# First tile of x in two channel halves, with offsets per stage and tile in the planner's ranks

## The chip, the cores and the metric

The kernel runs on one core of a Trainium2 chip. The metric is the device time of one execution in microseconds (us). The core has five engines, each with its own in-order instruction queue: TensorE (PE) for matrix products, VectorE (DVE) and ScalarE (ACT) for elementwise work, GpSimd (POOL), and SyncE (SP), which here only issues DMA transfers. PE writes to PSUM, and VectorE and ScalarE read it from there.

## The reference

A small neural speech codec: a depthwise convolution over time with three taps, SiLU, a residual vector quantiser with four codebooks of eight entries, and a second depthwise convolution over the sum of the chosen entries. `x` is 2 x 16000 x 512, in bf16.

```python
xp = jnp.pad(x, ((0,0),(pad,pad),(0,0)))
for i in range(K):                                  # K = 3
    z = z + xp[:, i:i+T, :] * dw_enc[i][None, None, :]
z = _silu(z)
res = z
for s in range(Nq):                                 # Nq = 4, C = 8 entries each
    cb = codebooks[s]
    d2 = |res|^2 - 2.0 * res @ cb.T + |cb|^2
    sel = cb[d2.argmin(-1)]
    q = q + sel
    res = res - sel
for i in range(K):
    y = y + qp[:, i:i+T, :] * dw_dec[i][None, None, :]
```

(The line for `d2` is written shorter here; `qp` is `q` padded like `xp`.)

## The kernel before

The 2 x 16000 time steps are cut into 18 tiles, numbered 0 to 17: 6, 8 and seven times 16 groups of 128 time steps for the first sequence, seven times 16, then 8 and 6 groups for the second. Time step and group are interleaved (`"(p g) d -> g p d"`), so that group g holds every G-th step, and the neighbour in time of a whole group is the group beside it. Channels lie on partitions: the 512 channels are four blocks of 128 (`KT` = 4).

**Loading** (`load`, L487). Every group is brought in by one transposing DMA from SyncE's queue (L493), 128 steps by 512 channels (128 KB), into slot g + 1 of the tile `XT[n % 2]`. Slots 0 and G + 1 are the halo: the last and the first group shifted by one step. For tiles inside a sequence they are two more transposing loads (L501, L507). For tile 0 both are made on GpSimd: a memset and a copy of slot G into slot 0 (L504), and a memset and a copy of slot 1 into slot G + 1 (L510). There are two `XT` buffers, so the loads of tile n + 2 come after the taps of tile n.

**Taps and SiLU** (`front`, L514, `front2`, L542). Each tile is worked in two channel halves h (blocks 0, 1 and 2, 3). Each half has six tap products `TA`/`TB` from `XT` and `WENC` (L531 on ScalarE or L532 on VectorE), two sums on VectorE (recorded at the helper's line, L364), exp on ScalarE (L537), plus one (L538 or L539), reciprocal on ScalarE (L549) and the gate `ZB * EX` on VectorE. The list `allx` (L524) names what a half's taps read; before, it is every slot of the tile.

**Selection** (`select`, L582; `resid`, L681). PE forms the products of z with the codebooks and with itself (L567); VectorE takes the scores (L601, L602) and decides three codebooks in a chain of small operations, with a PE transpose (L639), a copy of it (L643 on ScalarE or L644 on VectorE) and a correction on PE (L649) between them. The one-hot rows are transposed on PE (L672) and copied into `OHW` (L678, either engine). `resid` then subtracts the chosen entries from z in 24 pieces per tile. A piece taken by VectorE is one product group on PE (L701) and one add of PSUM to `ZB` (L709). A piece taken by ScalarE also needs `ZB` itself through an identity product (L700), and then one copy (L707). The fourth codebook follows (L725, L726, small operations, L672, L678).

**Back** (`back`, L741). PE multiplies the one-hot windows with prepared decoder weights (L758 to L762), ScalarE copies PSUM to `YB` (L766), and SyncE stores it (L789).

**Setup** (`setup`, L366) makes the constants with many short operations; up to the first tap VectorE is busy with them for 9.82 us, and the rest (decoder weights `WDEC`, L485, among it) lies between the work of tiles 0 and 1.

**The order.** Every step is registered with `add` under an engine (or both VectorE and ScalarE), a cost in us, a key of stage, tile number and place, and what it reads and writes. `Plan.order` (L75) simulates the engines with these costs. Again and again it takes the step that can start first; ties go to the smaller `rank` (L55), made of the tile number and two weights per stage in `WHEN`. There is one pair of weights each for tiles 0 to 2, 3 to 14 and 15 to 17 (`part`, L52). The result is the program order of all engines; `fill` (L807) puts filler products into PE where the plan sees it idle. Four things decide which engine a step gets:

- `SHARE`: a residual piece goes to VectorE if VectorE's load plus SHARE is below ScalarE's (L126).
- `QUOTA`: how many PSUM boxes may be held for an engine at a time (L120, L127). Score products also hold one for VectorE.
- `SLACK`: a step that both can do goes to ScalarE only if ScalarE would end no later than VectorE's end plus SLACK (L132).
- `LATENCY` and the PSUM banks' free times, from which the plan's waits follow.

These costs shape the order only; on the chip the queues wait for what they need.

## Time and profile before

| | |
|---|---|
| median of 8 runs (lowest to highest) | 732.79 us (728.52 to 735.04) |
| profiled execution: time, span | 731.26 us, 729.5 us |
| busy VectorE, ScalarE, PE (of which fillers, L809) | 674.8, 658.5, 590.6 us (72.8) |
| PE clock granted, mean | 0.967 |
| transposing loads, output stores (DMA instructions) | 283, 130 |
| issue of one transposing load, of one store (median) | 1.26 us, 0.36 us |
| first tap of tile 0, of tile 2 | 13.10 us, 52.35 us |
| last work of VectorE, of PE, of ScalarE | 719.8, 721.7, 724.1 us |

All times within the kernel count from the start of the span. A line such as "L709 DVE TENSOR_TENSOR ZB<-ZB,ps" is a group of instructions: source line, engine, operation, what is written from what, shapes and count; then the busy time, the mean duration of one in ns, and the engine's idle time just before them with what ended most of it. In a timeline the two first numbers are start and duration in us, and a bracket gives the idle time before. "SPq" is SyncE's queue issuing.

### The profile page before, as it was taken

The numbers are of one execution on the slowest core, as the hardware profiler recorded it, in microseconds if no ns is written. First come the engines' busy times: TensorE is split into PE (matmuls) and PEld (weight loads), VectorE is DVE, ScalarE is ACT, GpSimd is POOL, SyncE is SP. The second block draws the span as 40 slices with busy tenths as digits, with TensorE's granted clock in tenths as the row PEclk, the third lists the DMA queues.
The fourth block names the chain that finished last, engine by engine and source line by source line (L and its number), as shares of the span: only waits on it lengthen the run. The fifth ranks groups of instructions, "written<-read, shape, count | busy, mean of one in ns | idle before, by whom it ended". The sixth has DMA issues, their size and how long they took to land.

```text
span 729.5 us, 24386 instructions
## 1 busy us (share of the span) xinstructions
PE 590.6 (81%) x10725; PEld 288.4 (40%) x10725; DVE 674.8 (93%) x1258; ACT 658.5 (90%) x583; POOL 10.7 (1%) x35
## 2 busy tenths in 40 slices
PE   5977676887897886888788778877888897889995
PEld 2443243343443443434344334433344343444442
DVE  8779899999999999999998999999999999999993
ACT  6888998699999999899989999999899999999666
POOL 2000000000010000000000000000000010000000
PEclk9999799999999999999999999989999999999999
DMA  5454556624155353736634434542535130302316
GB/s 110 95 99 91 94 117 91 144 67 95 30 147 95 102 90 99 121 79 139 112 103 101 139 74 109 132 83 66 90 119 138 56 121 22 119 2 88 118 31 212
DMA packets 163968, 71.89 MB, mean 99 GB/s; under 512 B 155567, under 2 KB 155599, under 8 KB 163862
## 3 DMA queue, kind: packets, MB, share of 16 engines
q1 hardware_dynamic: 163646, 69.90, 41.3%
q8 instruction: 84, 1.38, 0.8%
q10 hardware_dynamic: 216, 0.43, 0.3%
q14 instruction: 22, 0.18, 0.1%
HBM read 0.43 MB, written 32.77 MB: 46 GB/s over the span
## 4 chain that ended last, share of the span: by engine, by line
DVE 51%; PE 26%; issue 8%; ACT 7%; SPq 6%; DMA 2%; DVEq 0%; ACTq 0%
DVE ZB L709 11%; PE ps L701 7%; DVE ZB L364 7%; DVE TA L364 7%; DVE TB L532 6%; PE ps L700 6%; SPq L493 6%; PE ps L567 4%; DVE TA L532 3%; PE ps L758 3%; DVE EX L539 2%; ACT YB L766 2%; DVE OHW L678 2%; PE ps L809 2%; ACT ZB L707 2%
## 5 line engine op out<-in xcount | busy, mean ns | idle before, releaser
L701 PE MATMUL ps<-OHW,CBN 128*128 128x512 bf16 (+1 forms) x768 | 267.2, 385 | 20.0 <-DVE ZB L709 10.3
L707 ACT CAST ZB<-ps 128x1024 bf16<-128x1024 f32 (+2 forms) x296 | 253.6, 932 | 31.5 <-PE ps L701 29.6
L700 PE MATMUL ps<-ZB,IDENT 128*128 128x512 bf16 (+1 forms) x530 | 205.5, 388 | 32.1 <-ACT ZB L707 14.0
L709 DVE TENSOR_TENSOR ZB<-ZB,ps 128x1024 bf16<-128x1024 bf16 (+2 forms) x136 | 143.2, 1065 | 3.9 <-PE ps L701 3.3
L701 PEld LDWEIGHTS <-CBN 128*128 128x128 bf16 x768 | 74.6, 99 | 142.4 <-issue 75.9
L766 ACT CAST YB<-ps 128x1024 bf16<-128x1024 f32 x126 | 121.8, 1044 | 9.4 <-PE ps L762 4.5
L537 ACT ACTIVATE EX<-ZB 128x4096 bf16<-128x4096 bf16 (+2 forms) x36 | 115.1, 3197 | 8.9 <-DVE ZB L364 8.6
L549 ACT ACTIVATE EX<-EX 128x4096 bf16<-128x4096 bf16 (+2 forms) x36 | 114.7, 3195 | 0.2
L567 PEld LDWEIGHTS <-ZB 128*32 128x32 bf16 x8064 | 75.3, 95 | 54.9 <-issue 52.7
L532 DVE TENSOR_SCALAR TB<-XT,WENC 128x2048 bf16<-128x2048 bf16 (+2 forms) x139 | 92.8, 686 | 0.2
L567 PE MATMUL ps<-ZB 128*32 128x64 bf16 x8064 | 87.6, 198 | 6.5 <-issue 4.2
L758 PE MATMUL ps<-WDEC,OHW 128*128 128x512 bf16 x252 | 74.0, 387 | 13.0 <-DVE ZB L709 4.6
L809 PE MATMUL ps<-MSK,IDENT 128*128 128x512 bf16 x294 | 72.8, 397 | 14.3 <-DVE RC L617 2.4
L700 PEld LDWEIGHTS <-IDENT 128*128 128x128 bf16 x530 | 52.8, 100 | 66.9 <-issue 14.7
L364 DVE TENSOR_TENSOR ZB<-ZB,EX 128x4096 bf16<-128x4096 bf16 (+2 forms) x36 | 72.7, 2022 | 3.6 <-ACT EX L549 3.6
L364 DVE TENSOR_TENSOR TA<-TA,TB 128x4096 bf16<-128x4096 bf16 (+2 forms) x36 | 72.8, 2022 | 1.0 <-ACT TB L531 0.6
L364 DVE TENSOR_TENSOR ZB<-TA,TB 128x4096 bf16<-128x4096 bf16 (+2 forms) x36 | 73.0, 2026 | 0.1
L532 DVE TENSOR_SCALAR TA<-XT,WENC 128x2048 bf16<-128x2048 bf16 (+2 forms) x70 | 46.9, 689 | 0.9 <-DMA out_dram<-YB 0.4
L809 PEld LDWEIGHTS <-IDENT 128*128 128x128 bf16 x294 | 28.7, 101 | 47.2 <-issue 19.2
L539 DVE TENSOR_SCALAR EX<-EX 128x4096 bf16<-128x4096 bf16 (+2 forms) x35 | 38.5, 1099 | 2.0 <-ACT EX L537 2.0
L758 PEld LDWEIGHTS <-OHW 128*128 128x128 bf16 x252 | 22.8, 98 | 41.3 <-issue 18.2
L561 PE MATMUL ps<-MSK,IDENT 128*128 128x512 bf16 (+1 forms) x64 | 24.5, 383 | 8.3 <-ACT ZB L707 2.4
(100 smaller groups left out, 401.5 us busy)
## 6 DMA issues: line engine op xcount, KB each, us to landing
out_dram<-YB SPq DMA_DIRECT2D x33, 448.0 KB
out_dram<-YB SPq DMA_DIRECT2D x28, 512.0 KB
XT<-in_x_dram SPq DMA_TRANSPOSE x283
out_dram<-YB SPq DMA_DIRECT2D x30, 60.0 KB
out_dram<-YB SPq DMA_DIRECT2D x31, 2.0 KB
out_dram<-YB SPq DMA_DIRECT2D x2, 224.0 KB
YB<-in_dw_dec_dram ACTq DMA_DIRECT2D x1, 384.0 KB
out_dram<-YB SPq DMA_DIRECT2D x1, 384.0 KB
```

The lines of the kernel that those rows point to most:

```text
L364: add("DVE", cost, key, lambda: nc.vector.tensor_tensor(out=out, in0=a, in1=b, op=op), reads, writes, **kw)
L532: lambda dst=dst, src=src, w=w: nc.vector.tensor_scalar(out=dst, in0=src, scalar1=w, scalar2=None, op0=ALU.mult),
L537: add("ACT", act(2 * R), ("exp", n, h), lambda: nc.scalar.activation(v(ex), Z, ACT.Exp, scale=-1.0), zt, [("EX", sl), "ACTTAB"], hold="E")
L549: nc.scalar.add_instruction(mybir.InstActivation(name=nc.get_next_instruction_name(), engine=mybir.EngineType.Activation, func=ACT.Reciprocal,
L567: nc.tensor.matmul(o[HB * q:HB * (q + 1), u * ZW:(u + 1) * ZW].rearrange("p (s c) -> p s c", s=2), lhsT=blk, rhs=both, start=False, stop=( ...
L700: nc.tensor.matmul(o, lhsT=IDENT, rhs=zg[:, k0:k0 + nk, :], start=True, stop=False)
L701: nc.tensor.matmul(o, lhsT=CBN[s, u][:, i * P:(i + 1) * P], rhs=W[:, k0:k0 + nk, PADC:PADC + P], start=not on_act, stop=True)
L707: nc.scalar.copy(zg, v)
L709: nc.vector.tensor_tensor(out=zg, in0=zg, in1=v, op=ALU.add)
L758: nc.tensor.matmul(o, lhsT=W[:, k, PADC:PADC + P], rhs=WDEC[u], start=True, stop=not wrap)
L766: add("ACT", act_psum(1024), key, lambda k=k, box=box, Y=Y, k0=k0: nc.scalar.copy(Y[:, 2 * (k - k0):2 * (k - k0) + 2, :].rearrange("p g d ...
L809: nc.tensor.matmul(PS[j // 2][:, 512 * (j % 2):512 * (j % 2) + NMK * ZW], lhsT=IDENT, rhs=MSK.rearrange("p u w -> p (u w)"), start=True, s ...
```

## The change

`load` takes tile 0 in two parts of two channel blocks each. For each part the load of slot G comes first, then slots 1 to G - 1, then both halo memsets and copies of that part; the second part follows the first. The tokens that order the steps now name slot and channel block, so that a half's taps depend on the loads of their own two blocks. For the other tiles the loads are as before. The planner gets the margins `MARGIN` (added to the latency behind PE, in front of PE and to the freeing of PSUM banks; a factor on the cost of products) and the table `NUDGE` with an offset per stage and tile, added to the ranks, to SHARE and to SLACK. `SHARE`, `SLACK`, `QUOTA` and `WHEN` have new values. What is computed is the same.

```diff
--- before.py
+++ after.py
@@ -27,9 +27,10 @@
     SPAN, BUSY = 3.413, 0.5
     GATE = {"resid": (1.0, 2.0), "back": (1.0, 2.0), "win0": (0.6, 1.5), "win3": (0.6, 1.5), "score0": (0.25, 1.4), "score3": (0.25, 1.4)}
 
-    def __init__(self, pairs, edges, share, slack, quota, when):
+    def __init__(self, pairs, edges, share, slack, quota, margin, when, nudge):
         self.steps, self.writer, self.readers = [], {}, {}
-        self.pairs, self.edges, self.share, self.slack, self.quota, self.when = pairs, edges, share, slack, quota, when
+        self.pairs, self.edges, self.share, self.slack, self.quota, self.margin, self.when = pairs, edges, share, slack, quota, margin, when
+        self.nudge = nudge
 
     def add(self, engine, cost, key, fn, reads=(), writes=(), take=None, free=None, hold=None, tail=0.0, after=(), dest=None, box=None, mm=0):
         n = len(self.steps)
@@ -54,7 +55,10 @@
 
     def rank(self, s):
         w = self.when[s["k"][0]][self.part(s)]
-        return w[0] + s["k"][1] + w[1] * s["k"][2]
+        return w[0] + s["k"][1] + w[1] * s["k"][2] + self.more(s["k"][0], s)
+
+    def more(self, name, s):
+        return self.nudge.get(name, (0,) * 99)[s["k"][1]] if s["k"][0] != "setup" and s["k"][1] >= 0 else 0.0
 
     def product(self, t, c, share, half):
 
@@ -123,13 +127,13 @@
                     if full:
                         dest = "ACT" if full[0] == "DVE" else "DVE"
                     else:
-                        dest = "DVE" if load("DVE", t) + self.share[self.part(s)] < load("ACT", t) else "ACT"
+                        dest = "DVE" if load("DVE", t) + self.share[self.part(s)] + self.more("share", s) < load("ACT", t) else "ACT"
                 elif dest and held[dest] >= self.quota[dest]:
                     return inf, None
                 kind = s["take"][0]
                 t = place(kind[dest] if isinstance(kind, dict) else kind, t)[0]
                 return t + late(many(s, dest), t, cost(s, dest) if s["dest"] == "ANY" else s["c"]), dest
-            if isinstance(s["e"], tuple) and e == "ACT" and t + s["c"]["ACT"] > max(at[s["n"]], clock["DVE"]) + s["c"]["DVE"] + self.slack[self.part(s)]:
+            if isinstance(s["e"], tuple) and e == "ACT" and t + s["c"]["ACT"] > max(at[s["n"]], clock["DVE"]) + s["c"]["DVE"] + self.slack[self.part(s)] + self.more("slack", s):
                 return inf, None
             if s["mm"]:
                 t += late(s["mm"], t, s["c"])
@@ -185,7 +189,7 @@
                 c += self.TABLE
             if s["mm"]:
                 m = many(s, dest)
-                c = self.product(t, c, *self.GATE.get(s["k"][0], (0.5, 1.5))) - t
+                c = self.product(t, c * self.margin[3], *self.GATE.get(s["k"][0], (0.5, 1.5))) - t
                 run += m
                 if run > self.CHUNK:
                     run -= self.CHUNK
@@ -198,11 +202,11 @@
                 if s["free"]["dest"]:
                     held[s["free"]["dest"]] -= 1
                 for j in s["free"]["banks"]:
-                    banks[j] = end + self.LATENCY[e]
+                    banks[j] = end + self.LATENCY[e] + self.margin[2]
             out.append(s)
             for u in users[n]:
                 ue = steps[u]["e"]
-                at[u] = max(at[u], t + c + self.AGAIN[e] if ue == e else end + self.LATENCY[e])
+                at[u] = max(at[u], t + c + self.AGAIN[e] if ue == e else end + self.LATENCY[e] + (self.margin[0] if e == "PE" else self.margin[1] if ue == "PE" else 0.0))
                 left[u] -= 1
                 if not left[u]:
                     open_(u)
@@ -242,17 +246,36 @@
     PAIR = 1
     NX, NE, NZ, NOH, NY = 2, 3, 4, 4, 4
     NA = 4
-    SHARE = (19.5, 1.71, -1.34)
-    SLACK = (0.8, -4.83, -5.72)
-    QUOTA = {"ACT": 4, "DVE": 4}
-    WHEN = {"setup": ((-0.05, 1.675), (0.613, 1.016), (0.464, 0.931)), "load": ((-2.074, 0.741), (-2.063, 0.601), (-2.58, 0.741)),
-            "pad": ((-1.343, 0.11), (-1.736, 0.115), (-2.291, 0.134)), "taps": ((0.284, 0.643), (-0.413, 0.648), (0.441, 1.172)),
-            "exp": ((0.672, 0.139), (0.624, 0.043), (0.853, 0)), "plus1": ((1.287, 0.521), (0.349, 0.234), (0.268, 0.646)),
-            "recip": ((0.542, 0.819), (0.469, 0.213), (1.361, 0.627)), "gate": ((-0.104, 0.712), (0.552, 0.521), (1.523, 0.809)),
-            "score0": ((-0.134, 0), (0.889, 0), (-0.19, 0)), "decide": ((1.83, 0.266), (-0.088, 0.293), (0.366, 0.69)),
-            "win0": ((2.039, 0), (2.077, 0), (2.756, 0)), "resid": ((1.585, 0.742), (1.683, 0.632), (1.826, 0.993)),
-            "score3": ((2.285, 1.086), (2.738, 0.327), (2.939, 1.624)), "decide3": ((1.327, 0.17), (2.815, 0.429), (3.624, 0.724)),
-            "win3": ((3.135, 0.143), (3.003, 1.197), (2.818, 0.209)), "back": ((2.723, 0.576), (3.156, 1.159), (4.372, 0.628))}
+    SHARE = (20.32, 2.45, -1.26)
+    SLACK = (0.55, -2.68, -0.35)
+    QUOTA = {"ACT": 4, "DVE": 3}
+    MARGIN = (0.11, 0.1, 0.09, 0.99)
+    WHEN = {"setup": ((-0.075, 1.733), (0.873, 1.153), (0.447, 1.29)), "load": ((-2.074, 0.741), (-2.063, 0.601), (-2.58, 0.741)),
+            "pad": ((-1.046, 0.11), (-1.746, 0.115), (-2.301, 0.134)), "taps": ((0.32, 0.593), (-0.433, 0.598), (0.548, 1.122)),
+            "exp": ((0.779, 0.02), (0.866, 0.292), (0.542, 0.02)), "plus1": ((1.574, 0.521), (0.401, 0.243), (0.499, 0.646)),
+            "recip": ((0.841, 0.843), (0.479, 0.099), (0.839, 0.513)), "gate": ((-0.651, 0.637), (0.045, 0.466), (1.326, 0.763)),
+            "score0": ((-0.134, 0), (0.831, 0), (1.042, 0)), "decide": ((1.32, 0.893), (-0.17, 0.631), (0.104, 1.108)),
+            "win0": ((1.017, 0.099), (1.541, 0.158), (1.696, 0.167)), "resid": ((1.523, 0.74), (1.683, 0.63), (1.735, 0.798)),
+            "score3": ((2.288, 1.101), (2.749, 0.339), (3.011, 1.624)), "decide3": ((1.558, 0.17), (2.848, 0.453), (4.276, 0.668)),
+            "win3": ((3.135, 0), (3.068, 1.159), (3.197, 0.216)), "back": ((2.796, 0.565), (3.449, 1.148), (4.029, 0.553))}
+    NUDGE = {"setup": (0, 0, 0, 0, 0.01, 0, 0, 0, 0, 0, 0, 0, 0, 0, 0.01, 0, 0, 0),
...
+             "pad": (0, 0, 0, 0, 0.01, 0, 0, -0.24, 0.12, 0, 0, 0, -0.23, 0, 0.01, 0, 0, 0),
...
+             "exp": (-0.48, -0.94, 0.01, -0.13, 0.01, 0.76, 0.35, -0.05, 0, 0, 0, 0, 0, 0, -0.13, 0, 0, 0),
...
+             "gate": (0, 0.06, 0, 0, -0.34, -0.78, 0, -0.02, 0, -0.23, 0, 0, 0, 0, 0, -0.02, 0, 0.46),
...
+             "decide": (0, 0, -0.1, 0, 0.06, 0.38, 0, 0, -0.18, 0, 0, 0.04, -0.62, 0, 0.1, 0, 0.43, 0.7),
+             "win0": (0, 0, -0.1, 0, 0.01, 0.05, 0, 0, 0.07, 0, 0, 0, 0, 0, 0.01, -0.41, 0, 0),
...
+             "share": (0.1, -3.6, 1.2, 0, -1, 0.5, 0, 0, 0, 0, 0, 0, 0, -0.1, 0, -0.7, 0.1, -0.4),
+             "slack": (2.1, 0, 0, 0, 0, 0, 0, -1.2, 0, 0, 0, 0, 0, 0, 0, -0.3, -0.3, 1.2)}
     assert B == len(SIZES) and T >= GM * P and GM <= 16
 
     xf = x.flatten_outer_dims()
@@ -322,7 +345,7 @@
     CBN = {(s, u): sb([P, D], BF16, f"CBN{s}_{u}") for s in range(3) for u in range(2)}
     WDEC = [sb([P, D], BF16, f"WDEC{v}") for v in range(4)]
 
-    plan = Plan(NA, (3, len(tiles) - 3), SHARE, SLACK, QUOTA, WHEN)
+    plan = Plan(NA, (3, len(tiles) - 3), SHARE, SLACK, QUOTA, MARGIN, WHEN, NUDGE)
     add = plan.add
 
     def ps(box):
@@ -486,28 +509,35 @@
 
     def load(st):
         n, G = st["n"], st["G"]
-        X = XT[n % NX]
-        src = xf[st["row0"]:st["row0"] + G * P, :].rearrange("(p g) d -> g p d", g=G)
-
-        def one(g):
-            nc.sync.dma_start_transpose(out=X[:, :, g + 1, :], in_=src[g])
-        for g in range(G):
-            add("SP", 1.56 if n < 2 else 1.36, ("load", n, 0.01 * g), lambda g=g: one(g), [], [("X", n % NX, g + 1)], tail=1.5)
+        X, xs = XT[n % NX], n % NX
+        r0, t0 = st["row0"], st["row0"] % T
+        src = xf[r0:r0 + G * P, :].rearrange("(p g) d -> g p d", g=G)
+        parts = 2 if n == 0 else 1
+        per = KT // parts
+        cost = (1.56 if n < 2 else 1.36) / parts
+
+        def fetch(slot, rows, part, at):
+            i = slice(per * part, per * (part + 1))
+            tok = [("X", xs, slot, i0) for i0 in range(KT)[i]]
+            add("SP", cost, ("load", n, at), lambda: nc.sync.dma_start_transpose(out=X[:, i, slot, :], in_=rows[:, per * P * part:per * P * (part + 1)]),
+                [], tok, tail=1.5)
+
         key = ("pad", n - 20 * (n == 0), 0)
-        xe, xo = [("XE", n % NX)], [("X", n % NX, G + 1)]
-        r0, t0 = st["row0"], st["row0"] % T
-        if t0 and n:
-            before = xf[r0 - 1:r0 - 1 + G * P, :].rearrange("(p g) d -> g p d", g=G)[0]
-            add("SP", 1.56 if n < 2 else 1.36, ("load", n, 0.01 * G), lambda: nc.sync.dma_start_transpose(out=X[:, :, 0, :], in_=before), [], xe, tail=1.5)
-        else:
-            pool_memset(X[:, :, 0, 0:2], 0.0, xe, 0.3, key)
-            add("POOL", 1.0, key, lambda: nc.gpsimd.tensor_copy(X[:, :, 0, 1:P], X[:, :, G, 0:P - 1]), [("X", n % NX, G)], xe)
-        if t0 + G * P < T and n:
-            behind = xf[r0 + 1:r0 + 1 + G * P, :].rearrange("(p g) d -> g p d", g=G)[G - 1]
-            add("SP", 1.56 if n < 2 else 1.36, ("load", n, 0.01 * G), lambda: nc.sync.dma_start_transpose(out=X[:, :, G + 1, :], in_=behind), [], xo, tail=1.5)
-        else:
-            pool_memset(X[:, :, G + 1, P - 2:P], 0.0, xo, 0.3, key)
-            add("POOL", 1.0, key, lambda: nc.gpsimd.tensor_copy(X[:, :, G + 1, 0:P - 1], X[:, :, 1, 1:P]), [("X", n % NX, 1)], xo)
+        for part in range(parts):
+            i = slice(per * part, per * (part + 1))
+            at = lambda slot: [("X", xs, slot, i0) for i0 in range(KT)[i]]
+            for g in ([G - 1] if n == 0 else []) + list(range(G - (n == 0))):
+                fetch(g + 1, src[g], part, 0.3 * part + 0.01 * g * (g < G - 1 or n > 0))
+            if t0 and n:
+                fetch(0, xf[r0 - 1:r0 - 1 + G * P, :].rearrange("(p g) d -> g p d", g=G)[0], part, 0.3 * part + 0.01 * G)
+            else:
+                pool_memset(X[:, i, 0, 0:2], 0.0, at(0), 0.3, key)
+                add("POOL", 1.0 / parts, key, lambda i=i: nc.gpsimd.tensor_copy(X[:, i, 0, 1:P], X[:, i, G, 0:P - 1]), at(G), at(0))
+            if t0 + G * P < T and n:
+                fetch(G + 1, xf[r0 + 1:r0 + 1 + G * P, :].rearrange("(p g) d -> g p d", g=G)[G - 1], part, 0.3 * part + 0.01 * G)
+            else:
+                pool_memset(X[:, i, G + 1, P - 2:P], 0.0, at(G + 1), 0.3, key)
+                add("POOL", 1.0 / parts, key, lambda i=i: nc.gpsimd.tensor_copy(X[:, i, G + 1, 0:P - 1], X[:, i, 1, 1:P]), at(1), at(G + 1))
 
     state = {}
 
@@ -521,7 +551,7 @@
         v = lambda t: t.rearrange("p i (b c) -> p i b c", c=P)
         Z = ZB[n % NZ][:, 2 * h:2 * h + 2, 0:G, :]
         zt = [("Z", n % NZ, i, u) for i in (2 * h, 2 * h + 1) for u in range(2)]
-        allx = [("X", xs, g) for g in range(1, G + 2)] + [("XE", xs)]
+        allx = [("X", xs, g, i) for g in range(G + 2) for i in (2 * h, 2 * h + 1)]
 
         key = ("taps", n, h)
         for k in range(K):
```

## Prediction

> **What bounds the kernel now.** I read the page from the top: busy shares, slices, chain. Then I asked for sums over stretches, for the SyncE queue and GpSimd in order of time, for the groups by shape and for the waits.
>
> ```profile
> PE 590.6 (81%) x10725; PEld 288.4 (40%) x10725; DVE 674.8 (93%) x1258; ACT 658.5 (90%) x583; POOL 10.7 (1%) x35
> ...
> DVE 51%; PE 26%; issue 8%; ACT 7%; SPq 6%; DMA 2%; DVEq 0%; ACTq 0%
> ```
>
> Two engines are nearly full at once, VectorE (DVE) and ScalarE (ACT). Half the chain of work that ended last is VectorE, and a visible 6% is SyncE's queue (SPq). The stretches (first pair: start and length; then busy PE, PEld, DVE, ACT, POOL) say where the idle time lies:
>
> ```profile
> 0.00:13.10 13.10, 4.66 (x22) 2.22 (x23) 9.82 (x58) 7.44 (x34) 3.91 (x29) 1.00 0.58 114
> 13.10:52.35 39.25, 34.42 (x382) 16.47 (x381) 30.94 (x82) 32.24 (x38) 0.00 (x0) 1.00 0.50 98
> ...
> 120.00:160.00 40.00, 33.19 (x429) 16.09 (x423) 37.07 (x71) 29.61 (x25) 0.00 (x0) 0.96 0.52 113
> ...
> 240.00:280.00 40.00, 32.48 (x658) 16.05 (x657) 39.77 (x59) 39.78 (x32) 0.91 (x2) 1.00 0.51 111
> 280.00:680.00 400.00, 331.55 (x6567) 163.11 (x6565) 382.74 (x678) 377.58 (x302) 3.16 (x2) 0.96 0.39 95
> 680.00:720.00 40.00, 37.61 (x661) 17.95 (x660) 35.05 (x93) 27.50 (x35) 0.00 (x0) 1.00 0.30 107
> ```
>
> Until 52.35 us, when the first taps of tile 2 run, VectorE is idle for 52.35 - 9.82 - 30.94 = 11.6 us. Adding up all stretches between 80 and 680 us gives VectorE 574.6 busy of 600 (25.4 idle) and ScalarE 562.9 (37.1 idle). So there ScalarE has some room and VectorE little, but 240 to 280 shows that both can be full for 40 us together. From 680 on ScalarE has 12.5 us of room while VectorE works.
>
> ```profile
> 0.74 18.90 SPq L493 DMA_TRANSPOSE XT<-in_x_dram  x14
> 19.68 1.26 SPq L501 DMA_TRANSPOSE XT<-in_x_dram  x1
> 20.99 1.26 SPq L507 DMA_TRANSPOSE XT<-in_x_dram  x1
> 22.38 21.96 SPq L493 DMA_TRANSPOSE XT<-in_x_dram  x16
> ...
> 47.07 22.88 SPq L493 DMA_TRANSPOSE XT<-in_x_dram  x16
> ```
>
> SyncE issues transposing loads without a gap: one per 1.31 us (0.74, 2.11, 3.40, 4.71 are starts in the chain), tiles 0 and 1 until 22.25, tile 2 until 46.95, and so on to 126 us. Early on the load queue sets the pace together with VectorE.
>
> ```profile
> 3.81 0.61 POOL L510 COPY XT<-XT 128x508 bf16<-128x508 bf16 x1 [1.96 <-DMA XT<-in_x_dram]
> ...
> 11.83 0.75 POOL L504 COPY XT<-XT 128x508 bf16<-128x508 bf16 x1 [6.10 <-DMA XT<-in_x_dram]
> ```
>
> The halo copy L510 ran 1.7 us after its source's issue ended (2.06), while later slots were still on their way: dependences go by region, so a tap that reads two channel blocks can wait for these alone. L504 waited for the sixth load (issued 7.88 to 9.15, so 2.7 us to landing), and the first tap follows at 13.10.
>
> ```profile
> L707 ACT CAST ZB<-ps 128x1024 bf16<-128x1024 f32 x234 | 224.1, 1028 | 21.6 <-PE ps L701 20.3 <-ACT ZB L707 0.9
> L700 PE MATMUL ps<-ZB,IDENT 128*128 128x512 bf16 x501 | 196.1, 391 | 30.1 <-ACT ZB L707 12.7 <-DVE ZB L709 12.4 <-DVE OHW L678 2.6
> L709 DVE TENSOR_TENSOR ZB<-ZB,ps 128x1024 bf16<-128x1024 bf16 x102 | 123.8, 1217 | 3.7 <-PE ps L701 3.3
> ```
>
> A residual piece costs VectorE 1.217 us, or ScalarE 1.028 us plus two identity products on PE. VectorE nearly never starves for one: 3.3 us in 5 waits.
>
> **The change part by part.** All terms are against the profiled execution: span 729.5, time 731.26, so 1.76 lies around the span. The median shown, 732.79, is 1.53 above it.
>
> *Halves of tile 0.* Six loads of 128 KB become twelve of 64 KB on SyncE's queue, and two memsets and two copies on GpSimd become four and four. No row shows a half transpose. Its issue lies between 0.36 us (the median issue of an output store, whatever its size) and 1.31 us (a whole one). The page counts 155567 packets under 512 B; over 283 transposes that is 550 each, and half the channels should need about half. Nearest is the transpose row itself, halved to 0.66, with something that does not shrink: I take 0.80. Twelve then last 9.6 us against 8.45 (0.74 to 9.19), so every later load moves back by 1.2 us; the ends are -4.1 and +7.3. The first half's sixth issue ends at 0.74 + 4.8 = 5.5 and lands 2.7 later, at 8.2. Its halo copies no longer come last, because their sources are issued first; the taps can start near 8.5 instead of 13.1.
>
> That is not 4.6 us of time. The setup work that VectorE does before 13.1 (9.82 us) must still be done, and tile 2 cannot be tapped before its loads land: 46.95 + 1.7 to 2.7 = 48.7 to 49.7, with the delay 49.9 to 50.9. Now it is tapped at 52.35, after waits of 2.1 us for tile 1's score products. If tile 0 and 1 run ahead by some microseconds, these waits go and tile 2 starts about 2 us earlier; some of the 3.2 us that VectorE idles between 52.35 and 80 goes too. I take -2.5 for the start. The bounds are -5 (a half at 0.36) and +3.9: at 1.31 tile 2's loads land at 56 to 57, 7.3 later, and only 3.4 of that is slack. GpSimd's new copies cost nothing: ONES (4.35, read by PE at 9.92) and the KEY fills (read at 36) queue with them and have 5 us of cover. If a copy held ONES up beyond 9.92, the delay would go straight into setup.
>
> Against this stands one rule. The Trainium skill, "DMA: Bandwidth & Descriptors", section "Rules for kernel authors", says to merge small transfers, since below 64 KB mostly overhead is paid. A half is exactly 64 KB; taken strictly, a half costs as much to issue as a whole and the start costs +3.9 where the row gives -2.5. I follow the row, because the issue rate of 1.31 us for 128 KB is 100 GB/s with the DMA engines half idle, so the issue and not the transfer is the limit here.
>
> *SHARE, SLACK and QUOTA.* In tiles 3 to 14 SHARE goes from 1.71 to 2.45, QUOTA for VectorE from 4 boxes to 3, SLACK from -4.83 to -2.68: all three send work from VectorE to ScalarE. One residual piece moved takes 1.217 from VectorE and adds 1.028 to ScalarE and 2 x 0.39 to PE (591 busy of 729, of which 72.8 are fillers). The idle times are equal after (37.1 - 25.4) / (1.217 + 1.028) = 5 pieces, which takes 6 us off VectorE. Part of ScalarE's idle time is waits for PE (19.0 us in 32 waits at L707 in this stretch) that stay, so I take -4.
>
> *Offsets per stage and tile, margins.* These set the order and, with the shares, which engine gets a piece; they add no instruction. What they can win is idle time on both engines: between 80 and 680 the mean is 31 us, and at the rate of 240 to 280 (0.23 in 40) it would be 3, so the bound is -28. The bound on the other side is as wide: new waits in an in-order queue. The largest single hole is ScalarE's 10.4 us between 120 and 160, of which 6.9 is one copy (L643) queued ahead of an exponential while it waits for PE. Such a copy on VectorE costs 0.22. I take -2, about one fifth of that hole on both engines.
>
> *The end.* SLACK for tiles 15 to 17 goes from -5.72 to -0.35, which lets ScalarE take copies of one-hot windows (L678, 0.35 to 0.70 us on VectorE) in its 12.5 us of room; but SHARE with its offsets is -1.96 for tile 15 and -1.66 for tile 17 (before -1.34), which keeps more pieces on VectorE at 0.55 to 1.2 each. Two or three copies off, one piece on: -1, bounds -4 and +3.
>
> The sum is -2.5 - 4 - 2 - 1 = -9.5: 731.26 - 9.5 = 721.8 by the profiled execution, 723.3 as a median.
>
> **The rivals.**
>
> *A. A half is issued at the price of a whole.* For it: all 283 issues show one price, so what part is fixed can't be seen. Against: the packets halve. Then start +3.9, the rest as above: -3.1, 729.7. The point is 0.99 us per half: (8.45 + 3.4) / 12, where tile 2's slack is used up. Chance 12%.
>
> *B. Slower: VectorE starves in the residual stage.* Score products also hold VectorE's boxes; with 3 boxes and two of them scores, one residual piece can be in hand, and VectorE waits for PE (L709 on L701). A wait there lasts 0.66 us now (3.3 / 5). The 7 us of gain outside the start are eaten by 11 further waits among the 97 such pieces between 80 and 680; at 22 the net is +5, 737.8. Against it: warm products start 0.21 us apart, so PE makes a piece in about 0.43 while VectorE needs 1.217, and two boxes would do. Chance 16%.
>
> *C. The new order only moves the waits.* The three middle and end terms vanish, and the start's 2.5 is lost again because both engines are full later: 732.8, give or take 2. For it: the in-order queues exchange one wait for another. Against: 37.1 and 25.4 us of idle time are there to be taken. Chance 11%.
>
> **How the numbers follow.** The forecast has 61%, with a range of its own of 716 to 729. Below it lies what the orders can win beyond my terms, above it A, C and B. I leave out the part of B above 738 and what lies below 712: range 712 to 738. A change of 0.3% (2.2 us) is about what a measurement can tell from none. Faster: 61% and nine of A's 12, with 1 or 2 from C, 72%. Same: the rest of A and most of C, 11%. Slower: B and a little of C, 17%.
>
> **What would show it.** Start: first tap between 8 and 9.5 us; half issues 0.7 to 0.9 apart; tile 2's first taps at 50 to 51. Middle: L709 on 128x1024 falls from 102 towards 95, L707 rises from 234, VectorE's busy time falls by 4 to 8 us, ScalarE's rises by 3 to 6, and L643's wait of 6.9 is gone. End: more of L678 on ScalarE after 680. Wrong would be: halves 1.3 apart (A), a long list of waits of L709 for L701 (B), or busy times moved as said with the idle time of both larger by as much (C).

## The result, and the profile after

| | before | after |
|---|---|---|
| median (lowest to highest), us | 732.56 (727.87 to 735.04), 32 runs | 739.41 (736.02 to 741.28), 11 runs |
| profiled execution: time, span, us | 731.26, 729.5 | 735.9, 733.8 |
| VectorE busy, idle within the span, us | 674.8, 54.7 | 671.0, 62.8 |
| VectorE idle before 80 us, from 80 to 680 us | 14.8, 25.4 | 20.5, 27.7 |
| transposing loads issued | 283 | 289 |
| first tap of tile 0, of tile 2, us | 13.10, 52.35 | 9.77, 55.70 |

The changed kernel is slower: the ratio is 1.0091, with a 95% interval of 1.0072 to 1.0109. The forecast was 723.3 us, faster, in a range of 712 to 738. It was wrong in its sign, and the time lies outside the range. The profiled execution of the kernel after is 3.5 us below its median, so the two profiles show 4.6 us of the 6.9.

Busy times first, from the page of the kernel after: the engines' totals, then the shares of the chain that ended last.

```profile
PE 592.1 (81%) x10712; PEld 288.9 (39%) x10712; DVE 671.0 (91%) x1251; ACT 663.6 (90%) x590; POOL 11.6 (2%) x39
...
DVE 44%; PE 22%; ACT 17%; issue 9%; SPq 4%; DMA 2%; ACTq 0%; DVEq 0%
```

VectorE lost 3.8 us of work and ScalarE gained 5.1, near what was forecast. All the same the span grew by 4.3. So the whole loss is idle time: VectorE's rose by 8.1, from 54.7 to 62.8. The stretches of the kernel after say where (start to end, length; busy PE, PEld, DVE, ACT, POOL with counts; then PE clock, DMA share, GB/s):

```profile
0.00:13.10 13.10, 0.98 (x10) 0.75 (x10) 7.70 (x40) 4.26 (x21) 3.45 (x26) 1.00 0.34 69
13.10:52.35 39.25, 28.41 (x222) 12.33 (x222) 28.37 (x85) 32.68 (x46) 1.07 (x7) 0.96 0.46 93
52.35:80.00 27.65, 22.98 (x322) 11.05 (x321) 23.39 (x50) 21.68 (x30) 0.00 (x0) 0.94 0.48 96
120.00:160.00 40.00, 35.60 (x431) 17.01 (x430) 39.66 (x74) 35.21 (x27) 0.00 (x0) 0.96 0.59 127
240.00:280.00 40.00, 35.93 (x687) 18.04 (x685) 39.05 (x67) 38.87 (x34) 0.37 (x2) 1.00 0.40 82
680.00:720.00 40.00, 36.82 (x658) 17.14 (x657) 36.38 (x102) 26.48 (x35) 0.00 (x0) 1.00 0.27 92
```

Up to 52.35 us VectorE is idle for 52.35 - 7.70 - 28.37 = 16.3 us (before: 11.6), up to 80 us for 20.5 (14.8). Two thirds of the new idle time lie in this first tenth of the run. The DMA share of the first 13.1 us fell from 0.58 to 0.34: the same bytes arrive at a lower rate. The hole of ScalarE between 120 and 160 us did become smaller (29.61 busy, now 35.21). Between 240 and 280 us the two engines were already full, and there they lost 1.6 us together. From 680 on ScalarE still has 13.5 us of room (12.5 before).

What makes the start late stands in the chain of SyncE's queue in order of time (start, length, what), kernel after:

```profile
0.74 1.30 SPq L522
...
2.10 1.22 SPq L522
...
3.37 1.24 SPq L522
...
15.46 1.24 SPq L522
...
28.90 1.26 SPq L522
```

Halves start 1.27 to 1.36 us apart (one of them 1.79). A whole load started every 1.31 us before. So a half occupies the queue as long as a whole. The twelve halves of tile 0 end at 15.46 + 1.24 = 16.70 us, where six wholes ended at 9.15. Tile 2's loads start after 28.90 + 1.26 = 30.16 us instead of at 22.38. Three timelines of the kernel after show the consequence: SyncE, two of GpSimd's halo copies, and VectorE's first tap of each half of tile 0 (start, duration, what, count, and in brackets the idle time before):

```profile
0.74 117.81 SPq L522 DMA_TRANSPOSE XT<-in_x_dram  x84
118.65 0.52 SPq L819 DMA_DIRECT2D out_dram<-YB  x1
```
```profile
3.28 0.39 POOL L535 COPY XT<-XT 128x254 bf16<-128x254 bf16 x1 [1.90 <-DMA XT<-in_x_dram]
...
11.08 0.39 POOL L535 COPY XT<-XT 128x254 bf16<-128x254 bf16 x1 [4.80 <-DMA XT<-in_x_dram]
```
```profile
9.77 0.42 DVE L562 TENSOR_SCALAR TA<-XT,WENC 128x768 bf16<-128x768 bf16 x1 [3.16 <-DMA XT<-in_x_dram]
...
18.06 0.42 DVE L562 TENSOR_SCALAR TA<-XT,WENC 128x768 bf16<-128x768 bf16 x1 [2.58 <-DMA XT<-in_x_dram]
```

The queue runs on without a pause until 118 us, so all the loads behind are issued later too. The halo copy of the first half runs at 3.28, since its source comes first; that of the second half has to wait for the seventh issue and runs at 11.08. The first half of tile 0 is tapped 3.3 us earlier than before (9.77 instead of 13.10), as the change promises. The second half is tapped only at 18.06, tile 2 at 55.70 (3.35 later than before), tile 3 at 80.99 (77.82 before), tile 4 at 106.85 (104.14) and tile 5 at 137.67 (136.28).

These later taps do not stand idle for their loads, however. In VectorE's list of waits over the whole run (what waits for what: us in total, times, longest), its waits for loads of `x` are these alone:

```profile
DVE TA L562 <- DMA XT<-in_x_dram: 5.7, 2, 3.2
```

They are the 3.16 and 2.58 us in the brackets above, one ahead of each half of tile 0. ScalarE's list has no such wait ahead of a tap. Tile 1's last load lands at 33.50 us, just ahead of its first VectorE tap at 33.72. So the halves hurt at tile 0 itself, where the second half comes late; that the loads of tile 2 are issued 7.8 us later is not what delays the taps of tile 2 here.

### The profile page after: what moved, and what is told of

Same layout as the page of the kernel before. It is cut to its first block, busy times and chain, and to the rows that moved or that the text cites. A ratio compares the mean times of both kernels' runs of the same rounds, so it can differ in the third digit from the quotient of the medians.

```text
span 733.8 us, 24364 instructions
## 1 busy us (share of the span) xinstructions
PE 592.1 (81%) x10712; PEld 288.9 (39%) x10712; DVE 671.0 (91%) x1251; ACT 663.6 (90%) x590; POOL 11.6 (2%) x39
## 2 busy tenths in 40 slices
DMA packets 164159, 71.87 MB, mean 98 GB/s; under 512 B 155759, under 2 KB 155791, under 8 KB 164054
## 3 DMA queue, kind: packets, MB, share of 16 engines
q8 instruction: 83, 1.36, 0.8%
## 4 chain that ended last, share of the span: by engine, by line
DVE 44%; PE 22%; ACT 17%; issue 9%; SPq 4%; DMA 2%; ACTq 0%; DVEq 0%
DVE ZB L739 10%; ACT ZB L737 8%; PE ps L731 8%; DVE ZB L387 7%; PE ps L730 6%; DVE TB L562 5%; SPq L522 4%; PE ps L597 4%; DVE TA L387 4%; ACT YB L796 4%; ACT EX L567 2%; DVE TA L562 2%; ACT EX L579 2%; DVE EX L569 2%; PE ps L839 2%
## 5 line engine op out<-in xcount | busy, mean ns | idle before, releaser
L737 ACT CAST ZB<-ps 128x1024 bf16<-128x1024 f32 (+2 forms) x298 | 257.4, 963 | 29.9 <-PE ps L731 26.3
L739 DVE TENSOR_TENSOR ZB<-ZB,ps 128x1024 bf16<-128x1024 bf16 (+2 forms) x134 | 140.2, 1062 | 7.1 <-PE ps L731 6.0
L796 ACT CAST YB<-ps 128x1024 bf16<-128x1024 f32 x126 | 124.8, 1058 | 7.5 <-PE ps L788 6.9
L788 PE MATMUL ps<-WDEC,OHW 128*128 128x512 bf16 x252 | 75.6, 391 | 11.2 <-DVE ZB L739 5.0
```

The source lines that it names most:

```text
L737: nc.scalar.copy(zg, v)
L739: nc.vector.tensor_tensor(out=zg, in0=zg, in1=v, op=ALU.add)
L788: nc.tensor.matmul(o, lhsT=W[:, k, PADC:PADC + P], rhs=WDEC[u], start=True, stop=not wrap)
L796: add("ACT", act_psum(1024), key, lambda k=k, box=box, Y=Y, k0=k0: nc.scalar.copy(Y[:, 2 * (k - k0):2 * (k - k0) + 2, :].rearrange("p g d ...
```

## The experiments

Three explanations stood against each other: (1) the price of the half loads, (2) the weight loads on ScalarE's queue, which in the kernel after wait for half loads, and (3) the tables, which change the order of the work. In the expectations "the order" is the program order that the planner gives out.

### The loads and the order, one without the other

**The order of after, tile 0 in six whole loads.** The steps of the second part stay in the plan but issue nothing.

```diff
-            add("SP", cost, ("load", n, at), lambda: nc.sync.dma_start_transpose(out=X[:, i, slot, :], in_=rows[:, per * P * part:per * P * (part + 1)]),
-                [], tok, tail=1.5)
+            def go():
+                if part == 0:
+                    nc.sync.dma_start_transpose(out=X[:, :, slot, :], in_=rows)
+            add("SP", cost, ("load", n, at), go, [], tok, tail=1.5)
```


> The changed kernel's program order on every engine, with tile 0 loaded by six whole transposes instead of twelve halves (halo sources still first). Theory H (a half costs a whole issue, and SyncE is 7.8 us late from then on): tile 2's loads start near 22.4 us instead of 30.35, and the time falls from 739.4 to 733 to 735. Rival T (the new order itself is what is slower): the loads move as said, but the time stays at 738 to 740.

Measured: 734.14 us, ratio 1.0034 (1.0009 to 1.0058). The halves alone are thus worth 1.0091 - 1.0034 = 0.57%, or 4.2 us (the two intervals together leave a doubt of about 0.3%); the tables and the order cost the other 2.5. Tile 2's loads start at 22.00 us, and tile 2 is tapped at 52.73 us, 3.0 earlier than with halves. Of these 3.0 us 2.5 stand already at tile 0, where VectorE's first tap of the second half runs at 15.56 instead of 18.06. The stretches of this run:

```profile
0.00:80.00 80.00, 52.13 (x562) 25.16 (x569) 61.41 (x177) 60.58 (x95) 3.91 (x31) 0.94 0.49 99
80.00:680.00 600.00, 485.96 (x9406) 244.40 (x9474) 574.07 (x976) 570.04 (x455) 7.18 (x6) 0.97 0.42 96
```

The profiled execution, 732.10 us, is the fastest of the ten and 2.0 below their median, so these idle times show less than the 2.5 us. From 80 to 680 us this order leaves VectorE 25.9 us idle (before: 25.4). It fills ScalarE's room, 30.0 idle instead of 37.1, and no time is won by it. Before 80 us VectorE is idle for 18.6 us (before: 14.8), although the first tap runs at 11.16 instead of 13.10. What grew most there is its wait for ScalarE's reciprocals ahead of the gates (first 80 us, kernel before and then this run):

```profile
DVE ZB L364 <- ACT EX L549: 3.6, 3, 2.4
...
DVE ZB L387 <- ACT EX L581: 7.8, 4, 2.9
```

**The order of before, tile 0 in halves.** Each whole load of tile 0 is issued as two halves; nothing else moves.

```diff
-            nc.sync.dma_start_transpose(out=X[:, :, g + 1, :], in_=src[g])
+            for i in ((0, 2), (2, 4)) if n == 0 else ((0, 4),):
+                nc.sync.dma_start_transpose(out=X[:, i[0]:i[1], g + 1, :], in_=src[g][:, P * i[0]:P * i[1]])
```


> The kernel before, its program order kept on every engine, with each whole transpose of tile 0 issued as its two channel halves one after the other. Theory H: twelve issues at 1.29 us, tile 2's loads start at 30 us, time 737 to 740 instead of 732.6. Rival T: the delay is hidden, 731 to 734.

Measured: 737.19 us, ratio 1.0079 (1.0053 to 1.0105), that is 5.8 us more. SyncE's timeline:

```profile
0.74 26.32 SPq L494 DMA_TRANSPOSE XT<-in_x_dram  x20
...
28.41 1.26 SPq L508 DMA_TRANSPOSE XT<-in_x_dram  x1
29.80 22.67 SPq L494 DMA_TRANSPOSE XT<-in_x_dram  x16
```

Six more instructions move tile 2's loads from 22.38 to 29.80 us, 7.4 us, with not one byte more. Tile 2's first tap moves from 52.35 to 57.76 (5.4 us), and the kernel by about as much. Explanation 1 is shown.

Nearly all of the 5.4 us are there before tile 2: VectorE's first tap of tile 0 runs at 18.77 instead of 13.59, 5.2 us later. The chain of work that ended last leads there in this run (start, length, what; L505 is the halo copy that needs the sixth group, L533 a tap):

```profile
13.81 1.49 SPq L494
...
15.34 2.38 DMA XT<-in_x_dram
...
17.85 0.90 POOL XT L505
...
18.77 0.42 DVE TA L533
```

No tap of a later tile stands idle for its loads in this run either.

### The weight loads

In the kernel after, ScalarE's queue issues the codebooks and the decoder taps late, and its first copy comes 6 us later than before (4.15):

```profile
0.76 0.61 ACTq L368 DMA_DIRECT2D WER<-in_dw_enc_dram  x1
4.51 0.33 ACTq L369 DMA_DIRECT2D CB<-in_codebooks_dram  x1
9.67 0.36 ACTq L372 DMA_DIRECT2D YB<-in_dw_dec_dram  x1
10.12 0.27 ACT L418 COPY CBT<-ps 128x32 bf16<-128x32 bf16 x2 [8.11 <-DMA XT<-in_x_dram]
```

Before, the two loads went out at 1.40 and 3.69 us. In both kernels they follow the load of ScalarE's function table. In these two experiments the table's load is moved behind all three weight loads:

```diff
-    nc.scalar.preload_act_table_set("natural_log_exp_and_others")
...
             nc.scalar.dma_start(out=WDBC, in_=wd_rows)
+        nc.scalar.preload_act_table_set("natural_log_exp_and_others")
```

**The kernel after with it.**

> The changed kernel with ScalarE's activation table load moved behind the three weight loads, so that the weight loads are assigned their completion semaphores ahead of the halves; codebooks are then issued near 1.4 us and decoder taps near 2 us, instead of 4.51 and 9.67. Twelve halves as in the changed kernel. Theory H (SyncE's lateness is the cost): 737 to 739.5. Rival L (the weight loads' waits behind half transposes, which hold ScalarE until 10.1 us, are the cost): 732 to 735.

Measured: 739.73 us, ratio 1.0122 (1.0067 to 1.0177), which holds the 1.0091 of the kernel after. The weights are issued at 1.38 and 1.78 us, and the first copy runs at 3.93, 6 us earlier. The time does not follow.

**Before with halves, and with it.**

> The kernel before with halves issued in pairs, and with the weight loads ahead of the activation table load. It pays SyncE's 7.8 us and no wait of the weight loads. Theory H: 736 to 739, at most 1.5 below the same kernel with the waits. Rival L: 732 to 734, as before the change. Rival T: 731 to 734 in both.

Measured: 737.18 us, ratio 1.0084 (1.0057 to 1.0110), against 737.19 without. As a cause of the loss explanation 2 is out. Two delays lie side by side there. VectorE's waits in the first 80 us, without the move (first two lines) and with it (last line):

```profile
DVE GR L412 <- PE ps L456: 4.4, 1, 4.4
...
DVE TA L533 <- POOL XT L505: 0.5, 1, 0.5
...
DVE TA L533 <- POOL XT L505: 5.1, 1, 5.1
```

L412 is a step of the setup that needs the codebooks. With the weights first its 4.4 us fall to 0.6, as in the kernel before, and the first tap waits 5.1 us for the halo copy instead; it runs at 18.41 instead of 18.77.

### The tables

**One rank moved by 0.01.** How much does any other order cost? The first weight of "resid" for tiles 3 to 14 goes from 1.683 to 1.673; by the kernel's own planner more than 1800 of 2925 steps then stand elsewhere.

```diff
-"resid": ((1.585, 0.742), (1.683, 0.632), (1.826, 0.993)),
+"resid": ((1.585, 0.742), (1.673, 0.632), (1.826, 0.993)),
```


> The kernel before with one rank weight moved by 0.01 (the residual stage of tiles 3 to 14, 1.683 to 1.673). The planner then puts 1844 of its 2925 steps at another place. Theory S (any change of the tables deals a new order, whose time scatters by about a per cent and, from a chosen order, mostly upwards): 733 to 745. Rival P (the time follows what the tables ask for, and this asks for nothing): 731 to 733.

Measured: 737.72 us, ratio 1.0089 (1.0059 to 1.0118). A change that means nothing costs 6 us. The planner's own end of the plan moves too, from 694.9 to 707.3 us (see the table further down).

**SHARE alone**, with the values of the change:

```diff
-    SHARE = (19.5, 1.71, -1.34)
+    SHARE = (20.32, 2.45, -1.26)
```


> The kernel before with the change's SHARE values alone (19.5 to 20.32, 1.71 to 2.45, -1.34 to -1.26). Theory P of the prediction: about five residual pieces go from VectorE to ScalarE in tiles 3 to 14, and the time falls by 2 to 4 us, to 728 to 730. Theory S: the plan's own balance keeps the split (136 of 432 pieces on VectorE before, 136 in the new plan), the order is a new one, and the time is 733 to 745.

Measured: 741.39 us, ratio 1.0132 (1.0090 to 1.0173). The group of residual pieces on VectorE, and the page's totals:

```profile
L722 DVE TENSOR_TENSOR ZB<-ZB,ps 128x1024 bf16<-128x1024 bf16 x102 | 123.2, 1216 | 4.3 <-PE ps L714 3.6 <-ACT ZB L720 0.3
```
```profile
PE 582.0 (79%) x10656; PEld 289.5 (39%) x10728; DVE 679.2 (92%) x1258; ACT 659.5 (89%) x583; POOL 10.0 (1%) x35
```

There are 102 pieces as before, where the forecast moved five. VectorE's busy time even rose by 4.4 us, but not its work: every group has as many instructions as before, and their durations added one by one are 765.2 us against 765.6. In these profiles neighbouring instructions of an engine overlap by about 0.085 us, which busy time counts once, and in this order fewer of them overlap (1023 instead of 1063). So the new order did not change who does what; the time is lost between the instructions, not in them. QUOTA from 4 to 3 was not run, because in the planner it changes the place of none of the 2925 steps.

### Fewer, larger loads

If an issue has one price whatever it carries, the opposite of the change should win: two groups in one transposing load of 256 KB. This needs the slots of `XT` ahead of the channel blocks, so that the taps read rows of 128 elements with gaps.

**The layout alone:**

```diff
-    XT = [sb([P, KT, GM + 2, P], BF16, f"XT{b}") for b in range(NX)]
+    XT = [sb([P, GM + 2, KT, P], BF16, f"XT{b}") for b in range(NX)]
...
-            nc.sync.dma_start_transpose(out=X[:, :, g + 1, :], in_=src[g])
+            nc.sync.dma_start_transpose(out=X[:, g + 1, :, :], in_=src[g])
```


> The kernel before with XT laid out slot first (slot, channel block, step), so that the taps read rows of 128 with gaps; order, loads and issue count unchanged. It is the reference for pair_loads. Strided taps at the same rate: 730 to 734. If a strided tap leaves VectorE's fast rate (0.75 us for 128x2048 now), it is far slower, 760 or more.

Measured: 732.41 us, ratio 1.0009 (0.9980 to 1.0038). The layout is free; a tap of 128 x 2048 on VectorE takes 0.748 us.

**The layout and paired loads, in the order of before:**

```diff
-            nc.sync.dma_start_transpose(out=X[:, g + 1, :, :], in_=src[g])
+            if g % 2 == 0:
+                nc.sync.dma_start_transpose(out=X[:, g + 1:g + 3, :, :].rearrange("p g i c -> p (g i) c"),
+                                            in_=rows[:, g:g + 2, :].rearrange("p g d -> p (g d)"))
```


> As layout_only, with two groups of tile n in one transpose (128 steps by 1024 channels, 256 KB), in the order of before: 155 transposes instead of 283. Theory H (the issue is paid per transpose, whatever its size between 64 and 256 KB): issues stay 1.3 us apart, tile 2's loads land near 35 us instead of 49, and the time falls 2 to 6 us below layout_only, to 726 to 730. Rival B (the issue grows with the bytes from 128 KB on): 2.5 us apart, and 731 to 733.

Measured: 727.76 us, ratio 0.9949 (0.9926 to 0.9971). With the halos there are 157 loads, not 155. SyncE's timeline:

```profile
0.74 11.95 SPq L496 DMA_TRANSPOSE XT<-in_x_dram  x7
12.73 1.26 SPq L505 DMA_TRANSPOSE XT<-in_x_dram  x1
...
20.39 12.10 SPq L496 DMA_TRANSPOSE XT<-in_x_dram  x8
```

The issue of a pair lasts 1.31 us in the median, but single ones take up to 3.15, so the first seven come 1.7 us apart on average. Tiles 0 and 1 are issued by 15.3 us instead of 22.25, and tile 2's loads now wait for their buffer. Its first tap comes at 51.46, hardly earlier than before, since the order on VectorE is still the one made for slow loads. So the gain lies mostly elsewhere than forecast: against the layout alone VectorE's idle time falls from 15.4 to 13.6 us before 80 us, and from 27.2 to 23.7 between 80 and 680. Which wait of the later stretch fell because of the loads was not traced.

**The same, with the planner told the price** (1.34 us for a pair; 1.31 for a halo load, not shown here), tables of before:

```diff
-            add("SP", 1.56 if n < 2 else 1.36, ("load", n, 0.01 * g), lambda g=g: one(g), [], [("X", n % NX, g + 1)], tail=1.5)
+            add("SP", 0.0 if g % 2 else 1.34, ("load", n, 0.01 * g), lambda g=g: one(g), [], [("X", n % NX, g + 1)], tail=2.2)
```


> Pair loads with the tables of before, but with the load cost in the planner set to what the chip showed (1.34 per pair, landing 2.2 later), so the order is dealt anew. The plan's own end time is 696.4. Theory M (the plan's end time tells how good an order is on the chip: 694.9 gave 731.7, 707.3 gave 737.7 and 741.4): 730 to 735. Theory S (a new order costs about a per cent whatever its plan says): 734 to 741.

Measured: 731.73 us, ratio 0.9993 (0.9961 to 1.0026). Tile 2 is tapped at 34.30 us and VectorE is idle for only 4.7 us before 80, yet nothing is won: its work rose from 674.8 to 679.8, ScalarE's idle time between 80 and 680 us went from 37.1 to 42.8, and the run ended no sooner.

**Tables searched for the paired loads.** The planner was run with many tables (the changed kernel's `NUDGE` included) and those with the earliest end of its own plan were kept; `pair_685` and `pair_680` are named after that end. The edit is in the tables alone:

```diff
-    SHARE = (19.5, 1.71, -1.34)
-    SLACK = (0.8, -4.83, -5.72)
+    SHARE = (14.877, 1.924, -0.594)
+    SLACK = (5.891, -6.081, -1.404)
...
-    NUDGE = {}
+    NUDGE = {"recip": (-0.27, -0.86, -0.33, 0.06, 0.35, -0.13, -0.11, -0.35, 0.03, -0.91, 0.5, 0.15, -0.25, 0.29, 0.37, 0.05, 1.2, -0.54),
...
```


> As pair_plan, with tables chosen by a random search over ranks, SHARE, SLACK and offsets for a small end time of the plan: 685.4. Theory M: about 0.5 to 0.75 of the 11 us appear, 723 to 729. Theory S: 734 to 741, no better than pair_plan.

Measured: 723.09 us, ratio 0.9862 (0.9799 to 0.9925).

> As pair_685, from another start of the search, with the plan's end time at 680.5. Theory M: 719 to 726, below pair_685 and below pair_loads (727.8). Theory S: 734 to 741.

Measured: 708.29 us, ratio 0.9667 (0.9617 to 0.9718), the best of all, faster than both kernels. It is 10.7 us below the range expected (719 to 726): 4.9 us of plan between the two searched tables became 14.8 us on the chip. Its totals from the page, its first 80 us, and its residual pieces on ScalarE:

```profile
PE 557.2 (79%) x10553; PEld 279.5 (40%) x10630; DVE 670.2 (95%) x1255; ACT 662.2 (94%) x586; POOL 7.9 (1%) x35
```
```profile
0.00:80.00 80.00, 50.95 (x527) 23.84 (x533) 74.34 (x176) 71.08 (x94) 3.82 (x29) 0.89 0.70 121
```
```profile
L740 ACT CAST ZB<-ps 128x1024 bf16<-128x1024 f32 x230 | 219.4, 1048 | 5.8 <-PE ps L734 5.0 <-DVE ZB L393 0.6
```

VectorE and ScalarE do about as much as in the kernel after (670.2 and 662.2 against 671.0 and 663.6), and the span is 27 us shorter. VectorE is idle for 5.7 us before 80 us, and ScalarE's waits ahead of its residual pieces are 5.8 us in all (before 21.6).

**The order of pair_680 with single loads of 128 KB** divides this gain:

```diff
-                nc.sync.dma_start_transpose(out=X[:, g + 1:g + 3, :, :].rearrange("p g i c -> p (g i) c"),
-                                            in_=rows[:, g:g + 2, :].rearrange("p g d -> p (g d)"))
+                for q in (g, g + 1):
+                    nc.sync.dma_start_transpose(out=X[:, q + 1, :, :], in_=rows[:, q, :])
```


> The order of pair_680 on every engine, with each pair of groups issued as two transposes of 128 KB again (283 issues). Nothing else differs. Theory H (the price is paid per issue and SyncE's queue sets the pace up to tile 5): the loads of the first six tiles end about 1.31 x 8 us per tile later, the first 80 us lose 8 us or more of VectorE's work, and the time goes from 708.3 to 716 to 728. Rival (the gain of pair_680 is the order alone): 708 to 711.

Measured: 725.0 us, ratio 0.9880 (0.9848 to 0.9912).

```profile
0.00:80.00 80.00, 44.82 (x407) 20.48 (x411) 61.85 (x161) 58.18 (x82) 3.81 (x29) 0.87 0.48 102
```

With the same order, 126 issues more cost 16.7 us; 12.5 of them are VectorE's idle time before 80 us (18.2 against 5.7). In this order tile 2 does wait for its loads: its first tap runs at 46.49 us instead of 34.77, after the longest of VectorE's waits for `x`:

```profile
DVE TA L565 <- DMA XT<-in_x_dram: 9.5, 2, 9.1
```

The other 8.3 us below the kernel before are the order's. An order that no plan had been made for these loads still wins 1.2%, so the tables of before are not the best that whole loads allow.

One comparison behind this section is of use by itself: the end of the planner's own plan (a sum of its costs, not a time of the chip) against the median measured.

| kernel | plan's end, us | measured ratio to before |
|---|---|---|
| pair_680 | 680.5 | 0.9667 |
| pair_685 | 685.4 | 0.9862 |
| before | 694.9 | 1 |
| pair_plan | 696.4 | 0.9993 |
| rank_001 | 707.3 | 1.0089 |
| share_only | 707.3 | 1.0132 |

Over these six the two columns rise together, but not in proportion: before and pair_plan can't be told apart on the chip, and rank_001 and share_only have the same plan's end and differ by 0.4%. The plan of the kernel after ends at 700.5 (its margins included), between pair_plan and rank_001, and its ratio without halves (1.0034) lies between theirs too. That plan books a half at 0.78 us.

## Why the prediction was wrong, point by point

**The half loads: the step that failed.** The forecast took 0.80 us for a half's issue, as half a row plus something that does not shrink, and got -2.5 us for the start. Measured are 1.29 us from start to start, and 4.2 us more (5.8 in the order of before). The issue price is rival A's, which was given 12%, and the loss is close to A's +3.9. The working had counted right that a half carries about half the packets: six instructions more brought only 155759 - 155567 = 192 packets more. But the price does not go by packets. The remark that the issue and not the transfer is the limit was right too, and should have spoken for A: if the queue is held by issuing and not by bytes, halving the bytes has no reason to shorten it.

The rule that was set aside for the row, the Trainium skill's "DMA: Bandwidth & Descriptors", section "Rules for kernel authors" (merge small transfers), had the sign right. On this queue the measurement goes further than the 64 KB named there: a load of 256 KB costs hardly more to issue (1.31 us in the median) than one of 64 KB (1.25).

**The first tap: nearly right, and worth nothing.** It was forecast at 8 to 9.5 us and came at 9.77. But the working follows the first half of tile 0 alone and has no term for the second, whose loads come last. With 0.80 us the twelve halves would have ended at 0.74 + 9.6 = 10.3 us; they ended at 16.70, and the second half was tapped at 18.06.

**Where the delay arises.** The forecast and A look for it at tile 2, whose loads A has 7.3 us late against 3.4 us of slack. The loads were that late (7.8 us), yet tile 2's first tap, at 55.70 us, does not stand idle for them, neither here nor in the order of before with halves. The delay is made at tile 0: 2.5 us at its second half, and 5.2 us at its first tap in the order of before. That A's +3.9 comes so near the 4.2 us is therefore partly luck. The reading that the load queue sets VectorE's pace early in the kernel before does not hold for the taps either: none of them stands idle for `x` there.

**SHARE, SLACK, QUOTA (-4): busy times right, gain absent.** VectorE's work fell by 3.8 us (forecast 4 to 8) and ScalarE's rose by 5.1 (3 to 6), but not by five residual pieces. Two of them left VectorE (136 to 134, about 2.5 us), with four copies of one-hot rows (35 to 31, about 1.8 us) and one "plus one" (about 1.2 us), while a tap came to it. SHARE alone moves no piece, and QUOTA alone moves no step in the plan, with the tables of before or of after. In the run without halves the freed 3.3 us on VectorE (671.5) became 4.0 us of idle time, 3.8 of it before 80 us.

**Offsets (-2) and end (-1): not seen.** The ScalarE copy that waited for 6.9 us now waits for 1.4, as asked for, and after 680 us one copy of one-hot windows lies on ScalarE (0.475 us). The sum of -4, -2 and -1 should have shown in the order of after with whole loads as -7; there it is +2.5 us. This is rival C's mechanism (busy times move, idle time grows), a little worse than its price of none. C was given 11% because idle time on both engines seemed to be there for the taking. The 0.01 of rank shows what was overlooked: this order is already a good one among its neighbours, though not the best (the order of pair_680 with single loads takes 725.0 us). The two small changes of a table that were run cost 0.9% and 1.3%.

**Rival B** has its sign and not its size. The groups by shape and the list of waits, kernel after:

```profile
L739 DVE TENSOR_TENSOR ZB<-ZB,ps 128x1024 bf16<-128x1024 bf16 x100 | 120.9, 1218 | 5.7 <-PE ps L731 4.9 <-PE ps L669 0.2
```
```profile
DVE ZB L739 <- PE ps L731: 6.0, 9, 1.7
```

Nine waits of 6.0 us stand where five of 3.3 stood; eleven more were needed to turn the sign.

**The chances.** A was joined only with the full gains of the tables, and C only with cheap halves. Both together, 732.8 + 3.9 = 736.7, was on no list, although nothing excluded it. With the tables' own loss it is what happened. Which single table value costs the 2.5 us is open. The runs show where some of them go, the waits for reciprocals before 80 us, and no more.

## What to carry to other kernels

Before a load is cut into parts, ask whether its queue is held by issuing or by bytes: where instructions stand back to back at one price, more of them delay everything behind, and fewer and larger ones are the change to try. Test a change of loads in a frozen order, and a change of order with frozen loads; here the order alone cost 0.34%, the halves alone 0.79%, and both together 0.91%. In these runs a table that feeds the planner was better judged by the end of its plan than by the step it is named after, and it was worth tuning again when the price of the loads changed.

## What was not expected of the hardware

- A transposing load holds SyncE's queue for 1.25 us with 64 KB, 1.26 with 128 KB and 1.31 with 256 KB (medians; single issues take up to 3.15).
- Weight loads on ScalarE's queue wait for transfers of `XT` that were issued on SyncE's queue: the codebooks go out at 4.51 instead of 1.40 us when tile 0 comes in halves, and at 1.38 when ScalarE's table load comes behind them. In the trace of the kernel after, the codebooks' load waits for the completion semaphore of the half issued at 2.10 us and then uses the same one; the decoder taps' load does so with that of the half issued at 7.22. It costs nothing that can be measured here.
- In one and the same order, pairs of 256 KB instead of loads of 128 KB raise the DMA share of the first 80 us from 0.48 to 0.70: the DMA engines had room for what the issuing queue held back.
